# Nine loads of q in 1 KB rows, transposed by float32 products (retention and SiLU block, one core)

## The chip, the cores and the metric

The kernel runs on one core of a Trainium2 chip. The metric is the device time of one execution in microseconds (us); of several runs the median is taken. Below, PE is the matrix engine (TensorE), DVE the vector engine, ACT the scalar engine, POOL the general engine (GpSimd) and SP the engine that issues the DMAs (SyncE).

## What is computed

```python
# q, k, v: (4, 8, 768, 64) float32; w_in: (512, 2048), w_out: (2048, 512), both float64 in memory
gamma = 1.0 - 2.0 ** (-5.0 - np.arange(H, dtype=np.float32))
scale = 1.0 / np.sqrt(D)
for t in range(S):
    state = gamma[None, :, None, None] * state + np.einsum('bhd,bhe->bhde', k[:, :, t], v[:, :, t])
    y[:, :, t] = scale * np.einsum('bhd,bhde->bhe', q[:, :, t], state)
x = y.transpose(0, 2, 1, 3).reshape(B * S, H * D)      # (3072, 512)
h = x @ w_in
g = h * (1.0 / (1.0 + np.exp(-h)))
out = g @ w_out
```

A linear recurrence over the positions of each batch entry and head, and then a two-layer network with SiLU on its 3072 rows.

## The kernel before, in words

**Units.** The recurrence is computed in chunks of 128 positions: 6 chunks by 4 batch entries make 24 units, numbered 0 to 23, chunk by chunk. A unit has a q, a k and a v of 8 heads x 128 positions x 64 numbers, 256 KB each. `load(name, n)` (L148) brings one into SBUF with the position on the partition and (head, number) along it, so that every row of the DMA is one head's 64 numbers, 256 B. Units 0 to 7 have a place of their own (`early`, tile kqv); from unit 8 on they go to the tiles kf, qf and vf, of which qf has two buffers and the others three. All DMAs are issued by SP, one after the other.

**Stages of a unit.** `stage_t(n)` (L461) transposes k and q on PE, each by four transposes of 128 positions x 128 columns (two heads of 64) against the identity matrix (L476), into one PSUM bank each (kp, qp); ACT copies a bank to SBUF (L477, kt and qt: 64 numbers of an even head on the lower 64 partitions, of the odd head on the upper 64, and pair of heads x position along a partition). `scale_k` (L411, L418) and `scale_q` (L420, L423) multiply by powers of gamma on DVE. `stage_s` (L498, L504) forms the sums of k and v, `stage_a` (L508, L514) the scores of k and q in quarters of 64x64, `steps_a` (L518) masks the scores (am, L522) and carries the state (mid, state), and `stage_y` (L543, product L562) forms y. A small POOL memset on `token` (L406) makes the second part of y wait for the first. `steps_y` (L599) and `split_x` (L625) copy y and split it in three parts that go through PE in a reduced float format (xt, L633, L636, L639).

**Weights.** `load_w` (L174) brings in a slice of w_in, 512 KB, by one DMA of 128 partitions (L186) and two of 64 (L188), all in rows of 1 KB; `early_slice` (L244) turns its float64 into float32 and splits it on ACT and DVE (L205 to L224, L121 to L129).

**First layer.** `P(n)` stands for `multiply(c, f)` (L729, L734), twelve products of 128x128 weights by 512 columns into the banks ha and hb, and `CL` for the steps that close it (L742: ACT L744, DVE L749, ACT L754); its result goes to DRAM (`put_g`, L757, L760).

**Order.** PE's instructions go in the order of the program throughout. Up to L976 the other engines and SP do so as well; this early order is written out by hand (L858 to L975): a line there names a unit's stage (T, K, SC, A, Q, YA, YB, X), a step of a weight slice (W), a product (P, CL) or a load. In it units 0 to 8 pass through their stages and the first products (0, 0), (0, 1), (0, 2) and (1, 0) are made. `T(n)` is `stage_t(n)`. Dummy products on zeros (`fill`, `narrow`, L317 and L323) stand in places where PE would wait. Loads stand some units ahead of their use: for instance k and q of unit 10 behind T(8), and v of unit 9 behind T(7). From unit 10 on `halves` (L674) calls the stages between the products of the first layer; units 10 to 12 (ROWS) are transposed in halves of 64 positions (L485). From unit 14 on q and k are transposed by DMA. Then the first layer runs to its end, and the second layer (L1088, L1102) reads its results back from DRAM and multiplies them with w_out.

Of the kernel before, what the change touches and what calls it, by code (L numbers as in the profile page):

```python
# [13 lines left out]
FP32 = mybir.dt.float32  # L14
# [4 lines left out]
AF = mybir.ActivationFunctionType  # L19
# [15 lines left out]
def kernel(  # L35
# [28 lines left out]
    nc = tc.nc  # L64
    B, H, S, D = q.shape
    DM, DF = moe_w_in.shape
    C = 128
    NC = S // C
    HP = H // 2
    KIN = DM // 128  # L70
    NF = DF // 128
# [18 lines left out]
    one = pool("one", 1)  # L90
# [48 lines left out]
    units = [(c, b) for c in range(NC) for b in range(B)]  # L139
    kqv = {"k": {}, "q": {}, "v": {}}  # L140
    EARLY = 2 * B

    FAR = 3 * B + 2
    ROWS = range(2 * B + 2, FAR - 1)
# [3 lines left out]
    def load(name, n):  # L148
        if n >= len(units):
            return  # L150
        c, b = units[n]
        src = {"k": k, "q": q, "v": v}[name]
        if n == 4 * B and name == "k":
            t = conv.tile([128, H, D], FP32, tag="wl", name=f"kf_{n}")
            nc.sync.dma_start(out=t, in_=src[b, :, ds(c * C, C)].rearrange("h t d -> t h d"))
            kqv[name][n] = t
            return
        if n < EARLY:

            if n not in early:  # L160
                early[n] = wpool.tile([128, 3, H, D], FP32, tag=f"w{4 + n}", name=f"kqv_{n}")
            t = early[n][:, "kqv".index(name)]
        else:
            t = ld.tile([128, H, D], FP32, tag=f"{name}f", name=f"{name}f_{n}",
                        bufs=2 if name == "q" else 3)
        nc.sync.dma_start(out=t, in_=src[b, :, ds(c * C, C)].rearrange("h t d -> t h d"))  # L166
        kqv[name][n] = t


# [4 lines left out]
    def load_w(i):  # L174
        if i >= 2 * NF:
            return
        if wide:
            t = stage.tile([128, 2 * DM], U32, tag="wf", name=f"wf_{i}")
            w_in, w_out, n = moe_w_in.bitcast(U32), moe_w_out.bitcast(U32), 256
        else:  # L180
            t = stage.tile([128, DM], FP32, tag="wf", name=f"wf_{i}")
            w_in, w_out, n = moe_w_in, moe_w_out, 128
        if i < NF:
            to = t.rearrange("p (i o f) -> o p i f", o=2, f=n)
            src = w_in[:, ts(i, n)].rearrange("(i o p) f -> o p i f", o=2, p=128)
            nc.sync.dma_start(out=to[0], in_=src[0])  # L186
            for j in range(2):
                nc.sync.dma_start(out=to[1, ts(j, D)], in_=src[1, ts(1 - j, D)])  # L188
        else:
            nc.sync.dma_start(out=t, in_=w_out[ts(i - NF, 128), :])  # L190
        staged[i] = t
# [61 lines left out]
    evac, held, w_sb = [], [], {}  # L253
# [59 lines left out]
    def fill(out, n, start=True):  # L313

        cols = out.shape[-1] // 128
        for _ in range(n):
            nc.tensor.matmul(out, lhsT=zero, rhs=zero.unsqueeze(1).to_broadcast([128, cols, 128]),  # L317
                             start=start, stop=True, skip_group_check=True)

    def narrow(out, n):  # L320

        for _ in range(n):
            nc.tensor.matmul(out[:, :32], lhsT=zero, rhs=zero[:, :32], start=True, stop=True,  # L323
                             skip_group_check=True)

    for n in range(EARLY - 2):
        for name in "kqv":
            load(name, n)
        if n in (0, 3):
            load_w(n // 3)  # L330


    ident = const.tile([128, 128], FP32, tag="ident", name="ident")
# [19 lines left out]
    lgc = const.tile([128, HP], FP32, tag="lgc", name="lgc")  # L353
# [29 lines left out]
    xt, kt, qt, am = {}, {}, {}, {}  # L383
# [8 lines left out]
    def banks(tag, name, n=2):  # L392
        return ps_u.tile([128, n, 512], FP32, tag=tag, name=name)
# [3 lines left out]
    def turn(name):  # L397
        turns[0] += 1
        return ps_h.tile([128, 512], FP32, tag=f"h{turns[0] % 3}", name=name)
# [58 lines left out]
    FILL_FENCE = {0: 2, 2: 2, 3: 2}  # L458
    FILL_P = {(0, 0): 1, (1, 0): 2}

    def stage_t(n):  # L461

        src = kqv["k"][n], kqv["q"].pop(n)
        tp = turn(f"kp_{n}"), banks("q", f"qp_{n}", 1)[:, 0]

        def new(name, to, bufs):
            to[n] = one.tile([128, HP, C], FP32, tag=name, name=f"{name}_{n}", bufs=bufs)
            return to[n]

        made = ("kt", kt, 2), ("qt", qt, 3)  # L470
        if n not in ROWS:
            for i in range(2):
                fill(tp[i], FILL_T.get(n, (0, 0))[i])
                t = tp[i].rearrange("p (a t) -> p a t", a=HP)
                for a in range(HP):
                    nc.tensor.transpose(t[:, a, :], src[i][:, 2 * a : 2 * a + 2, :], ident)  # L476
                evac[:] = [nc.scalar.copy(out=new(*made[i]), in_=t).ins]  # L477
                if n in NARROW_T:
                    narrow(idle[0], NARROW_T[n][i])
            return  # L480
        tp = [t.rearrange("p (i a t) -> p i a t", i=2, a=HP) for t in tp]
        for i in range(2):
            for a in range(HP):
                for o in range(2):
                    nc.tensor.transpose(tp[o][:, i, a, :], src[i][ts(o, D), 2 * a : 2 * a + 2, :],  # L485
                                        ident[ts(o, D), ts(o, D)])
        made = [new(*m) for m in made]
        for o in range(2):
            for i in range(2):
                evac[:] = [nc.scalar.copy(out=made[i][:, :, ts(o, D)], in_=tp[o][:, i]).ins]  # L490
# [326 lines left out]

    sa, ys, asteps, ysteps = {}, {}, {}, {}

    def T(n):  # L820
        stage_t(n)

    def SC(n):
        sa[n] = sc, sums = score_tile(n)
        stage_s(n, sums)
        stage_a(n, sc)
        asteps[n] = steps_a(n, sc, sums)

    def A(n):
        next(asteps[n], None)  # L830

    def YA(n):
        ys[n] = stage_y(n)
        ys[n][0]()
        ys[n][1](0)

    def YB(n):
        ys[n][1](1)
        ysteps[n] = steps_y(n, ys[n][2])

    def X(n):
        next(ysteps[n], None)
# [3 lines left out]
    def W(i, times=1):  # L846
        if i not in slices:
            slices[i] = early_slice(i)
        for _ in range(times):
            next(slices[i], None)  # L850

    def loads(n):
        for name in "kqv":
            load(name, n)

    K, Q = scale_k, scale_q

    idle[:] = [banks("y", "idle")[:, 0]]  # L858
    narrow(idle[0], 39)
    fill(idle[0], 2)  # L860
    narrow(idle[0], 39)
    T(0), K(0)
    nc.scalar.activation(out=token, in_=lgc[:1, :1], func=AF.Silu)
    SC(0), A(0), Q(0), A(0), A(0)
    W(0), W(0), W(0), W(0), W(0)
    YA(0), YB(0), X(0)
    T(1), K(1)
    W(0)
    load_w(2)
    W(0)  # L870
    X(0), X(0)
    SC(1), A(1)
    W(0)
    A(1)
    Q(1), A(1)
    T(2), K(2)
    W(0), X(0)
    W(0), W(0)
    YA(1), SC(2)
    A(2)  # L880
    YB(1), X(1)
    A(2), Q(2), A(2)
    X(1)
    T(3), K(3)
    X(1), X(1)
    YA(2), YB(2), X(2)
    SC(3), A(3), A(3), Q(3), A(3)
    X(2), W(1), W(1)
    X(2), X(2)
    YA(3), YB(3), X(3), X(3)  # L890
    W(1), W(1)
    T(4)
    X(3), X(3)
    K(4)
    W(1), W(1)
    loads(EARLY - 2), loads(EARLY - 1)
    closing = {}

    def P(n):
        c, f = divmod(n, NF)  # L900
        closing[n] = close_steps(c, f, *multiply(c, f))

    def CL(f):
        next(closing[f], None)

    def KA(n):
        t = kqv["k"][n]
        for h in range(H):
            nc.scalar.activation(out=t[:, h, :], in_=t[:, h, :], func=AF.Copy,
                                 scale=gk[:, units[n][0], h : h + 1])  # L910

    P(0)
    next_chunk()
    SC(4)
    CL(0), CL(0), CL(0)
    put_g(0)
    W(1)
    T(5)
    A(4), A(4), Q(4), K(5), A(4)
    W(1), W(1)  # L920
    YA(4), SC(5), YB(4)
    loads(EARLY)
    load_w(3)
    W(2), W(1)
    A(5)
    W(1), W(2), W(2)
    X(4)
    T(6)
    P(1)
    A(5), Q(5), A(5)  # L930
    KA(6)
    W(2), W(2), W(2)
    load("k", EARLY + 1), load("q", EARLY + 1)
    load_w(4)
    W(2)
    CL(1), CL(1)
    W(2)
    YA(5), SC(6), YB(5)
    X(5)
    W(2), W(2)  # L940
    A(6)
    W(2)
    CL(1)
    put_g(0)
    T(7)
    P(2)
    load("v", EARLY + 1)
    K(7), A(6), Q(6), A(6)
    X(4), X(5), X(4), X(4)
    CL(2)  # L950
    YA(6), SC(7), YB(6)
    X(6)
    T(8)
    load("k", EARLY + 2), load("q", EARLY + 2)
    A(7), A(7), Q(7)
    next_chunk()
    K(8), A(7)
    CL(2), CL(2)
    put_g(0)
    X(5), X(5)  # L960
    X(6)
    YA(7), SC(8), YB(7)
    X(7), X(7)
    A(8)
    X(6), X(6)
    T(9)
    load("v", EARLY + 2), load("k", EARLY + 3), load("q", EARLY + 3)
    X(7), X(7)
    A(8), Q(8), A(8)
    P(NF)  # L970
    KA(9)
    CL(NF), CL(NF)
    taken[0] = 3
    begin_w()
    CL(NF)  # L975
# [179 lines left out]
```

## Time and profile before

| | |
|---|---|
| runs | 613.5, 613.05 and 611.95 us, median 613.05 |
| span of the profiled execution, from the first instruction to the last (the profile gives no other time of it) | 612.6 us |
| PE, busy | 600.9 us (98%) |
| weight loads of PE | 495.9 us (81%) |
| DVE, busy | 397.1 us (65%) |
| ACT, busy | 324.5 us (53%) |
| DMA | 144,336 packets, 108.90 MB, of them 101,137 under 512 B |
| granted clock of PE | full throughout |

How to read it: the profile's page gives for each engine the time in which it has an instruction running; PE's instructions are pipelined and their ends modelled, so a busy PE can still have waits in it. The slices cut the span in 40 equal parts of 15.3 us and give the busy share of each in tenths, 9 being 90% or more; the DMA row is the mean share of 16 DMA engines, and can go over 1 in a short stretch. In a timeline a row has start, duration, engine, line, operation, output and inputs; "PEld" is a weight load of PE, "SPq" an issue by SP. The chain of waits is the work that ended last, followed back from the end. A wait row says which engine and line waited for which: us in total, how often, the longest.

### The profile page before, as it was taken

The numbers are of one execution on the slowest core, as the hardware profiler recorded it, in microseconds if no ns is written. First come the engines' busy times: TensorE is split into PE (matmuls) and PEld (weight loads), VectorE is DVE, ScalarE is ACT, GpSimd is POOL, SyncE is SP. The second block draws the span as 40 slices with busy tenths as digits, with TensorE's granted clock in tenths as the row PEclk, the third lists the DMA queues.
The fourth block names the chain that finished last, engine by engine and source line by source line (L and its number), as shares of the span: only waits on it lengthen the run. The fifth ranks groups of instructions, "written<-read, shape, count | busy, mean of one in ns | idle before, by whom it ended". The sixth has DMA issues, their size and how long they took to land.

```text
span 612.6 us, 13713 instructions
## 1 busy us (share of the span) xinstructions
PE 600.9 (98%) x5509; PEld 495.9 (81%) x5509; DVE 397.1 (65%) x672; ACT 324.5 (53%) x598; POOL 32.9 (5%) x89
## 2 busy tenths in 40 slices
PE   8898999999999999999999999999999999999997
PEld 6686788888888888888888888888888888888886
DVE  4797898678886676766689774635545463645631
ACT  7688678678676667676698632212221322313211
POOL 3000020100021111210000000000000000000000
PEclk9999999999999999999999999999999999999999
DMA  9999976586799699998777542623524433433301
GB/s 195 209 199 231 258 214 203 160 254 188 258 231 233 154 263 263 258 291 255 248 249 267 169 138 69 206 69 106 169 72 136 137 110 97 152 123 99 107 1 69
DMA packets 144336, 108.90 MB, mean 178 GB/s; under 512 B 101137, under 2 KB 109585, under 8 KB 144273
## 3 DMA queue, kind: packets, MB, share of 16 engines
q1 hardware_dynamic: 144272, 108.03, 62.3%
q8 instruction: 43, 0.70, 0.5%
q14 instruction: 21, 0.16, 0.1%
HBM read 66.06 MB, written 36.70 MB: 168 GB/s over the span
## 4 chain that ended last, share of the span: by engine, by line
PE 92%; DMA 3%; SPq 2%; DVE 2%; issue 1%; ACT 0%; DVEq 0%
PE ha L734 28%; PE o L1088 21%; PE oa L1088 14%; PE hb L734 14%; PE ob L1088 7%; PE y L562 3%; DMA qf<-in_q_dram 2%; PE sc L504 1%; SPq L166 1%; PE sc L514 1%; DMA kqv<-in_v_dram 1%; SPq L188 1%; PE o L1102 0%; PE oa L1102 0%; PE kp L485 0%
## 5 line engine op out<-in xcount | busy, mean ns | idle before, releaser
L734 PE MATMUL ha<-xt,wi 128*128 128x512 f32 x768 | 193.0, 393 | 0.0
L734 PEld LDWEIGHTS ha<-xt,wi 128*128 128x128 f32 x768 | 142.4, 188 | 30.5 <-DVE xt L636 0.2
L1088 PE MATMUL o<-wo,gs 128*128 128x512 f32 x564 | 143.1, 389 | 0.0
L805 ACT ACTIVATE gs<-gr 128x512 fp32r<-128x512 f32 x96 | 53.2, 621 | 139.0 <-issue 138.0
L1088 PEld LDWEIGHTS o<-wo,gs 128*128 128x128 f32 x564 | 105.9, 188 | 22.0
L807 DVE TENSOR_TENSOR gs<-gr,gs 128x512 fp32r<-128x512 f32 x96 | 62.1, 684 | 94.2 <-ACT gs L805 94.2
L1088 PE MATMUL oa<-wo,gs 128*128 128x512 f32 x376 | 115.7, 389 | 0.0
L749 DVE TENSOR_TENSOR g<-g,hb 128x512 f32<-128x512 f32 x96 | 65.7, 684 | 57.6 <-ACT g L744 42.6
L734 PE MATMUL hb<-xt,wi 128*128 128x512 f32 x384 | 102.7, 389 | 0.0
L734 PEld LDWEIGHTS hb<-xt,wi 128*128 128x128 f32 x384 | 72.1, 188 | 15.1
L1088 PEld LDWEIGHTS oa<-wo,gs 128*128 128x128 f32 x376 | 70.5, 188 | 14.6
L754 ACT ACTIVATE g<-g 128x512 f32<-128x512 f32 x96 | 60.3, 629 | 37.7 <-DVE g L749 37.6
L1088 PE MATMUL ob<-wo,gs 128*128 128x512 f32 x188 | 73.1, 389 | 0.0
L744 ACT ACTIVATE g<-ha 128x512 f32<-128x512 f32 x96 | 56.7, 591 | 28.6 <-PE ha L734 19.8
L808 DVE SCALAR_TENSOR_TENSOR gs<-gs 128x512 fp32r<-128x512 f32 x96 | 62.0, 683 | 0.1
L1088 PEld LDWEIGHTS ob<-wo,gs 128*128 128x128 f32 x188 | 35.3, 188 | 7.4
L205 ACT ACTIVATE ca<-wf 128x512 f32<-128x512 f32 x32 | 21.6, 675 | 6.6 <-DVE cs L218 4.0
L522 DVE TENSOR_TENSOR am<-sc,decay 128x512 f32<-128x512 f32 x24 | 16.5, 687 | 11.4 <-PE sc L514 11.4
L1112 ACT ACTIVATE o<-o 128x512 f32<-128x512 f32 x10 | 6.0, 598 | 33.4 <-PE o L1088 33.0
L218 DVE SCALAR_TENSOR_TENSOR cs<-ca,cs 128x512 uint32<-128x512 uint32 x32 | 22.7, 710 | 0.9
L639 DVE SCALAR_TENSOR_TENSOR xt<-xt 128x512 fp32r<-128x512 f32 x28 | 19.9, 715 | 0.7
L562 PE MATMUL y<-qt,mid 64*64 64x64 f32 x376 | 19.4, 220 | 0.4 <-issue 0.4
(122 smaller groups left out, 562.2 us busy)
## 6 DMA issues: line engine op xcount, KB each, us to landing
gd<-g SPq DMA_DIRECT2D x96, 256.0 KB, 3.7
gr<-gd SPq DMA_DIRECT2D x96, 256.0 KB, 2.7
wf<-in_moe_w_out_dram SPq DMA_DIRECT2D x16, 512.0 KB, 4.7
out_dram<-o SPq DMA_DIRECT2D x23, 256.0 KB, 2.1
wf<-in_moe_w_in_dram SPq DMA_DIRECT2D x16, 256.0 KB, 4.6
wf<-in_moe_w_in_dram SPq DMA_DIRECT2D x32, 128.0 KB, 4.1
kf<-in_k_dram SPq DMA_DIRECT2D x16, 256.0 KB, 4.1
qf<-in_q_dram SPq DMA_DIRECT2D x16, 256.0 KB, 4.1
```

The costliest lines, as they stand in the source:

```text
L205: top = nc.scalar.activation(out=a.bitcast(FP32), in_=hi.bitcast(FP32), func=AF.Abs, scale=2.0 ** -3).ins
L218: nc.vector.scalar_tensor_tensor(out=s, in0=a, scalar=3, in1=s, op0=ALU.logical_shift_left, op1=ALU.bitwise_xor)
L562: i = nc.tensor.matmul(to[ts(e, D), o, a, :], lhsT=lhsT, rhs=rhs, start=key not in started, stop=True, skip_group_check=True).ins
L639: nc.vector.scalar_tensor_tensor(out=x[2], in0=x[1].bitcast(FP32), scalar=-1.0 / EPS, in1=x[0].bitcast(FP32), op0=ALU.mult, op1=ALU.add)
L734: nc.tensor.matmul(hb if i == 2 else ha, lhsT=w_sb[f][:, i, ts(kk, 128)], rhs=xt[c][:, i, kk, :], start=kk == 0 and i != 1, stop=kk == KIN ...
L744: copied[:] = [nc.scalar.activation(out=hs, in_=ha, func=AF.Copy, scale=ONE_E).ins]
L749: taken_out[:] = [nc.vector.tensor_tensor(out=hs, in0=hs, in1=hb, op=ALU.subtract).ins]
L754: nc.scalar.activation(out=hs, in_=hs, func=AF.Silu)
L805: nc.scalar.activation(out=t[:, 0, :], in_=g, func=AF.Copy, scale=HALF)
L807: nc.vector.tensor_tensor(out=t[:, 1, :], in0=g, in1=high, op=ALU.subtract)
L808: nc.vector.scalar_tensor_tensor(out=t[:, 2, :], in0=t[:, 1, :].bitcast(FP32), scalar=-1.0 / EPS, in1=high, op0=ALU.mult, op1=ALU.add)
L1088: nc.tensor.matmul(o, lhsT=g, rhs=wo[f][:, i, :], start=f == 0 and i != 1, stop=f == NF - 1 and i != 0)
```

## The change

Units 1 to 9 are called PACKED; R is 128 x 4 / 128 = 4. Their q is loaded by two DMAs, one for the even heads (j = 0) and one for the odd (j = 1). A partition now holds four consecutive positions of one head of each kind: partition p = 4 u + a holds, at j, positions 4u to 4u + 3 of head 2a + j. Four positions of a head are 1 KB in DRAM, so each DMA moves 128 rows of 1 KB. The loads of k and v, and those of q in other units, stay.

`stage_t` is divided for units 0 to 9 in `stage_k` and `stage_q`, called one after the other where stage_t was called (`T` still names the two). For a packed unit, `stage_q` makes eight float32 products in place of four transposes. For every r (position within the four) and j the 128 partitions x 64 numbers are the weights, and the identity matrix is the moving operand, its columns taken in the order a, u, with a step of four numbers (16 bytes). The output, 64 partitions (lower half for j = 0, upper for j = 1) x 128 columns, goes to PSUM at a x 128 + 4u + r, again in steps of four numbers, so that the bank holds what the transposes left there, and the copy to SBUF is the same. `stage_t` stays for units from 10 on.

The order of all stages, steps and loads written out by hand is unchanged; the lines are only written one call to a line.

```diff
+    PACKED, R = {1, 2, 3, 4, 5, 6, 7, 8, 9}, C * HP // 128
...
-        nc.sync.dma_start(out=t, in_=src[b, :, ds(c * C, C)].rearrange("h t d -> t h d"))
+        rows = src[b, :, ds(c * C, C)]
+        if name == "q" and n in PACKED:
+            rows = rows.rearrange("(a j) (u r) d -> j u a (r d)", j=2, r=R)
+            for j in range(2):
+                nc.sync.dma_start(out=t[:, ts(j, R)].rearrange("p r d -> p (r d)"), in_=rows[j])
+        else:
+            nc.sync.dma_start(out=t, in_=rows.rearrange("h t d -> t h d"))
...
+    def stage_k(n):
+
+        src, u = kqv["k"][n], turn(f"kp_{n}")
+        fill(u, FILL_T.get(n, (0, 0))[0])
+        t = u.rearrange("p (a t) -> p a t", a=HP)
+        for a in range(HP):
+            nc.tensor.transpose(t[:, a, :], src[:, 2 * a : 2 * a + 2, :], ident)
+        evac[:] = [nc.scalar.copy(out=new_t(n, "kt"), in_=t).ins]
+        narrow(idle[0], NARROW_T.get(n, (0, 0))[0])
+
+    def stage_q(n):
+
+        src = kqv["q"].pop(n)
+        to, u = new_t(n, "qt"), banks("q", f"qp_{n}", 1)[:, 0]
+        fill(u, FILL_T.get(n, (0, 0))[1])
+        t = u.rearrange("p (a t) -> p a t", a=HP)
+        if n in PACKED:
+            to_r = u.rearrange("p (a u r) -> p r a u", a=HP, r=R)
+            for r in range(R):
+                for j in range(2):
+                    nc.tensor.matmul(to_r[ts(j, D), r], lhsT=src[:, j * R + r, :],
+                                     rhs=ident.rearrange("p (u a) -> p a u", a=HP),
+                                     start=True, stop=True, skip_group_check=True)
+        else:
+            for a in range(HP):
+                nc.tensor.transpose(t[:, a, :], src[:, 2 * a : 2 * a + 2, :], ident)
+        evac[:] = [nc.scalar.copy(out=to, in_=t).ins]
+        narrow(idle[0], NARROW_T.get(n, (0, 0))[1])
...
+    TK, TQ = stage_k, stage_q
+
     def T(n):
-        stage_t(n)
+        TK(n), TQ(n)
```

More of the change, by code (lines that the diff above doesn't have):

```diff
@@ L324, in narrow @@
                              skip_group_check=True)
[L326 to L330, printed above, removed]
+    load("k",0)
+    load("q",0)
+    load("v",0)
+    load_w(0)
+    load("k",1)
+    load("q",1)
+    load("v",1)
+    load("k",2)
+    load("q",2)
+    load("v",2)
+    load("k",3)
+    load("q",3)
+    load("v",3)
+    load_w(1)
+    load("k",4)
+    load("q",4)
+    load("v",4)
+    load("k",5)
+    load("q",5)
+    load("v",5)
     ident = const.tile([128, 128], FP32, tag="ident", name="ident")
@@ L459, with new_t @@
     FILL_P = {(0, 0): 1, (1, 0): 2}
+    def new_t(n, name):
+        made, bufs = (kt, 2) if name == "kt" else (qt, 3)
+        made[n] = one.tile([128, HP, C], FP32, tag=name, name=f"{name}_{n}", bufs=bufs)
+        return made[n]
+    def stage_k(n):
[23 more added lines that the diff above has]
+        narrow(idle[0], NARROW_T.get(n, (0, 0))[1])
     def stage_t(n):
@@ L472, in stage_t @@
             for i in range(2):
-                fill(tp[i], FILL_T.get(n, (0, 0))[i])
                 t = tp[i].rearrange("p (a t) -> p a t", a=HP)
@@ L477, in stage_t @@
                 evac[:] = [nc.scalar.copy(out=new(*made[i]), in_=t).ins]
-                if n in NARROW_T:
-                    narrow(idle[0], NARROW_T[n][i])
             return
@@ L856 @@
     K, Q = scale_k, scale_q
[L858 to L896, printed above, removed]
     closing = {}
@@ L910, in KA, with warm @@
                                  scale=gk[:, units[n][0], h : h + 1])
+    def warm():
+        nc.scalar.activation(out=token, in_=lgc[:1, :1], func=AF.Silu)
+    idle[:] = [banks("y", "idle")[:, 0]]
+    narrow(idle[0], 39)
+    fill(idle[0], 2)
+    narrow(idle[0], 39)
+    TK(0)
+    TQ(0)
+    K(0)
+    warm()
+    SC(0)
+    A(0)
+    Q(0)
+    A(0)
+    A(0)
+    W(0)
+    W(0)
+    W(0)
+    W(0)
+    W(0)
+    YA(0)
+    YB(0)
+    X(0)
+    TK(1)
+    TQ(1)
+    K(1)
+    W(0)
+    load_w(2)
+    W(0)
+    X(0)
+    X(0)
+    SC(1)
+    A(1)
+    W(0)
+    A(1)
+    Q(1)
+    A(1)
+    TK(2)
+    TQ(2)
+    K(2)
+    W(0)
+    X(0)
+    W(0)
+    W(0)
+    YA(1)
+    SC(2)
+    A(2)
+    YB(1)
+    X(1)
+    A(2)
+    Q(2)
+    A(2)
+    X(1)
+    TK(3)
+    TQ(3)
+    K(3)
+    X(1)
+    X(1)
+    YA(2)
+    YB(2)
+    X(2)
+    SC(3)
+    A(3)
+    A(3)
+    Q(3)
+    A(3)
+    X(2)
+    W(1)
+    W(1)
+    X(2)
+    X(2)
+    YA(3)
+    YB(3)
+    X(3)
+    X(3)
+    W(1)
+    W(1)
+    TK(4)
+    TQ(4)
+    X(3)
+    X(3)
+    K(4)
+    W(1)
+    W(1)
+    load("k",6)
+    load("q",6)
+    load("v",6)
+    load("k",7)
+    load("q",7)
+    load("v",7)
     P(0)
@@ L914 @@
     SC(4)
-    CL(0), CL(0), CL(0)
+    CL(0)
+    CL(0)
+    CL(0)
     put_g(0)
     W(1)
[L918 to L922, printed above, removed]
+    TK(5)
+    TQ(5)
+    A(4)
+    A(4)
+    Q(4)
+    K(5)
+    A(4)
+    W(1)
+    W(1)
+    YA(4)
+    SC(5)
+    YB(4)
+    load("k",8)
+    load("q",8)
+    load("v",8)
     load_w(3)
-    W(2), W(1)
-    A(5)
-    W(1), W(2), W(2)
-    X(4)
-    T(6)
-    P(1)
-    A(5), Q(5), A(5)
+    W(2)
+    W(1)
+    A(5)
+    W(1)
+    W(2)
+    W(2)
+    X(4)
+    TK(6)
+    TQ(6)
+    P(1)
+    A(5)
+    Q(5)
+    A(5)
     KA(6)
-    W(2), W(2), W(2)
-    load("k", EARLY + 1), load("q", EARLY + 1)
+    W(2)
+    W(2)
+    W(2)
+    load("k",9)
+    load("q",9)
     load_w(4)
     W(2)
-    CL(1), CL(1)
-    W(2)
-    YA(5), SC(6), YB(5)
-    X(5)
-    W(2), W(2)
+    CL(1)
+    CL(1)
+    W(2)
+    YA(5)
+    SC(6)
+    YB(5)
+    X(5)
+    W(2)
+    W(2)
     A(6)
@@ L944 @@
     put_g(0)
-    T(7)
-    P(2)
-    load("v", EARLY + 1)
-    K(7), A(6), Q(6), A(6)
-    X(4), X(5), X(4), X(4)
+    TK(7)
+    TQ(7)
+    P(2)
+    load("v",9)
+    K(7)
+    A(6)
+    Q(6)
+    A(6)
+    X(4)
+    X(5)
+    X(4)
+    X(4)
     CL(2)
-    YA(6), SC(7), YB(6)
-    X(6)
-    T(8)
-    load("k", EARLY + 2), load("q", EARLY + 2)
-    A(7), A(7), Q(7)
+    YA(6)
+    SC(7)
+    YB(6)
+    X(6)
+    TK(8)
+    TQ(8)
+    load("k",10)
+    load("q",10)
+    A(7)
+    A(7)
+    Q(7)
     next_chunk()
-    K(8), A(7)
-    CL(2), CL(2)
+    K(8)
+    A(7)
+    CL(2)
+    CL(2)
     put_g(0)
-    X(5), X(5)
-    X(6)
-    YA(7), SC(8), YB(7)
-    X(7), X(7)
-    A(8)
[L965 to L969, printed above, removed]
+    X(5)
+    X(5)
+    X(6)
+    YA(7)
+    SC(8)
+    YB(7)
+    X(7)
+    X(7)
+    A(8)
+    X(6)
+    X(6)
+    TK(9)
+    TQ(9)
+    load("v",10)
+    load("k",11)
+    load("q",11)
+    X(7)
+    X(7)
+    A(8)
+    Q(8)
+    A(8)
     P(NF)
     KA(9)
-    CL(NF), CL(NF)
+    CL(NF)
+    CL(NF)
     taken[0] = 3
```

## The prediction, made before the changed kernel was run

> **What bounds the kernel now.** I read the page's slices first, then the busy time of two stretches, then who waits for whom in the first of them.
>
> ```profile
> span 612.6 us, 13713 instructions
> ...
> PE   8898999999999999999999999999999999999997
> ...
> DMA  9999976586799699998777542623524433433301
> ```
>
> ```profile
> 0.00:60.00 60.00, 52.11 (x1338) 41.96 (x1339) 45.05 (x83) 45.86 (x113) 5.50 (x49) 1.00 0.93 208
> 60.00:600.00 540.00, 540.00 (x4131) 446.73 (x4131) 349.20 (x584) 276.38 (x482) 27.44 (x40) 1.00 0.60 177
> ```
>
> After the times in the second fence: PE, weight loads, DVE, ACT, POOL, granted clock, DMA share, GB/s. From 60 us on PE never rests: whatever comes late or early by then moves the end by as much, and nothing else does. The change touches only the stage before, units 1 to 9; its last transposes of q are at 53 us. There PE rests 60 - 52.1 = 7.9 us and the DMA engines are 93% busy. The waits of that stage which a faster load could end, from two windows (0 to 18 us, then 48 to 60 us):
>
> ```profile
> PE sc L504 <- DMA kqv<-in_v_dram: 1.6, 2, 1.1
> ...
> PE qp L476 <- DMA kqv<-in_q_dram: 0.3, 1, 0.3
> ```
>
> ```profile
> PE kp L485 <- DMA qf<-in_q_dram: 1.1, 1, 1.1
> ...
> PE kp L485 <- DMA kf<-in_k_dram: 0.3, 1, 0.3
> PE qp L476 <- DMA qf<-in_q_dram: 0.3, 1, 0.3
> ```
>
> In the timeline these are: q of unit 1 at 11.66 (0.31), v of unit 2 at 17.73 (1.12), q of unit 9 at 52.73 (0.26), k of unit 10 at 56.98 (0.34) and q of unit 10 at 58.54 (1.09). Unit 0's wait for v comes before any changed load. So **at most 3.1 us can be won**. The rest of PE's rest is dependence on DVE and ACT, and waits put down to "issue".
>
> **The loads.** A q load is 1024 rows of 256 B now and 256 rows of 1 KB after. Two stretches with nearly one kind of row each (256 B, then the 1 KB rows of w_in):
>
> ```profile
> 12.50:16.50 4.00, 4.00 (x117) 3.21 (x117) 3.35 (x7) 2.93 (x6) 0.00 (x0) 1.00 1.18 237
> 101.80:103.20 1.40, 1.40 (x8) 1.17 (x7) 1.40 (x3) 0.93 (x2) 0.00 (x0) 1.00 0.40 127
> ```
>
> At share 1 that is 237/1.18 = 201 and 127/0.40 = 317 GB/s, so 262 KB take 1.30 and 0.83 us: 0.47 us less a load. Two changed loads lie ahead of v of unit 2 (0.9 us), nine ahead of unit 10 (4.2 us). SP issues two DMAs instead of one:
>
> ```profile
> 70.89 0.39 SPq L166 DMA_DIRECT2D qf<-in_q_dram  x1
> ...
> 77.84 1.26 SPq L188 DMA_DIRECT2D wf<-in_moe_w_in_dram  x2
> ```
>
> The nearest row for a 128 KB half is L188, 1.26/2 = 0.63 us; two cost 1.26 + 0.04 between them against 0.39 when nothing is backed up, 0.9 us more, nine times 8.2 us. I take zero: before 60 us the same instruction takes 0.6 to 2.4 us because the DMA engines are behind, and a unit's k, q and v need 0.39 + 1.30 + 0.39 = 2.1 us of SP against 1.30 + 0.83 + 1.30 = 3.4 us of DMA. Were that cover gone, SP would eat the 4.2 us and unit 10 would land as late as now. The q load of unit 10 also needs the buffer of unit 8, which stage_q frees; that comes at about 51 us (below), and 4.1 us to landing gives 55, ahead of its use.
>
> **The products.** The rows, from the chain of waits:
>
> ```profile
> 18.42 0.47 PE sc L514 x32
> ...
> 19.11 0.59 PE kp L476 x4
> ...
> 19.91 0.44 PE qp L476 x4
> ```
>
> Gone: four transposes of 128 columns, 0.44 us, 0.11 each. Added: eight float32 products, 128 rows by 64 columns of weights, 128 columns moving. L514 shows what a float32 product is: 16 calls give 32 instructions, so each is two; 32 take 0.47 us, 14.7 ns each. In the timeline such products start in fours (y at 33.74 to 33.76, 33.80 to 33.82, 33.86 to 33.88), one in each 64x64 quarter every 58 ns. An instruction of 64 columns thus holds its quarter 58 ns; one of 128 columns 0.11 us, as the transposes do. Sixteen of them, two halves of the array side by side, take 8 x 0.11 = 0.88 us. Lower bound: 0.44, if the second pass hid; a gain is excluded, since no more columns stream at once than now. Upper bound: 1.76 without pairing, the same if pairing holds but the 16-byte steps (ident read, PSUM written) halve the rate, 3.5 with both. I take 0.88, because the paired quarters are the nearest row: **+0.44 us a unit**.
>
> Two more switches of array shape: kp costs 0.59 where it follows 64x64 products and 0.44 (qp) where it follows its own shape, so 0.15 a switch. Every unit gets one (k to q); units 4, 6, 7 and 9 a second, since a 128x128 product P follows. So +0.59 for units 1, 2, 3, 5 and 8, +0.74 for 4, 6, 7 and 9: 5.9 us in all. The copy to SBUF (0.58 us, contiguous as before) is unchanged.
>
> The Trainium skill (PSUM — Partial Sum Buffer, Specifications) says that any non-contiguous access pattern slows matmuls significantly; no row here has one, and by it the block is 1.76 us or more. The Trainium skill (TensorE: Matmul & The Clock Gate, Terms) has transposes four times as fast as float32 products; the rows above give 0.11 against 2 x 0.11 for 128 columns, so the trace says twice; by four it would again be 1.76, and its chance is in the first rival's.
>
> **What lies on the path.** Lateness of PE against the trace, walked unit by unit:
> - Units 1, 2: +0.59 - 0.31 (q lands sooner), then +0.59: scores of unit 2 could start at 16.61 + 0.9 = 17.5. v lands at 17.7 - 0.9 = 16.8. So 0.2 early.
> - Unit 3: +0.59, less the 0.17 that the next product waits for mid: 0.2 late. Unit 4: +0.74, 0.95 late.
> - Unit 5: +0.05 only; the products behind it wait for DVE (am, then qt L423) until 33.63. 1.0 late.
> - Unit 6: +0.74; the products behind P wait 0.35 for ACT L909 at 39.73, which itself moves some 0.1: +0.5. 1.5 late.
> - Unit 7: +0.74, 2.2. Unit 8: +0.59 less 0.1 ahead of qt: 2.7.
> - Unit 9: +0.74, less 0.26 (its q) and 0.25 (ha waits for xt L636 at 54.53): 2.95.
> - Unit 10: the waits of 0.34 and 1.09 are gone: 1.5 late.
> Then instructions: 24 more PE instructions a unit, 216 with their loads, on about 2700 before 60 us (1338 + 1339). The "issue" waits of PE between 21 and 52 us are 0.39, 0.43, 0.35 and 0.27; 8% more of 1.44 us is 0.12; as such a wait comes whole or not at all, I take 0.2. Together **+1.7 us**. The profiled execution has a span of 612.6 us, and no other time of it is given; the median of the runs is 613.05, so I add the difference there: 614.8 us. What a measurement of this kernel can tell from no change is about 0.3%, 1.84 us.
>
> **Rivals.**
> - *The steps of 16 bytes, or halves that don't pair* (0.32): the block takes 1.76 us, 0.88 more than in the sum. For: no row shows a strided operand of PE, nor two 128x64 tiles. Against: four quarters do run at once, and float32 streams at half the rate of L734 (512 columns in 1.85/8 = 0.23 us), which leaves time for a step. 9 x 0.88 = 7.9 us more, with some 0.5 hidden at units 6 and 8: 614.8 + 7.4 = 622.2. This is the Trainium skill's PSUM rule at work. Both together (0.04) give 16 us more still.
> - *Not slower: the landing of unit 10 sets the end* (0.15). The price is the block: at 0.44 us with the switches hidden in the "issue" waits, the waits won are 0.9 (v), 0.26, 0.34 and 1.09 = 2.6 us: 610.5. For: the chain runs through one piece of 11.8 us of q loads up to 58.5, and mostly through DVE from 30.7 to 44. Against: PE has no rest from 36 to 48 us. Linear between -2.6 (nothing added) and +1.5 (0.66 a unit), it decides at 0.42 a unit: less is faster.
> - *The rows of 1 KB do not land sooner* (0.05): SP's 0.9 us a load, or two DMAs' fixed costs, eat the 4.2 us. Unit 2 is 0.2 later than in the sum, unit 9's 0.26 stays; unit 10's waits still go, as PE arrives 3 us later. 613.05 + 2.2 = 615.3.
>
> **Chances.** Forecast 0.44, with its own range 613.0 to 616.8 (the walk's hidden parts, 2.4 us, half lost or half more found): faster 0.01, same 0.23, slower 0.20. Strided or unpaired 0.36 with both together, all slower. Landing 0.15: faster 0.12, same 0.03. No gain 0.05: same 0.03, slower 0.02. Sums: faster 0.13, same 0.29, slower 0.58. The range: from 611.2 (most of the landing case) to 622.5 (the strided case's middle); below lie 0.07, above 0.13.
>
> **What would show it.** Loads: packets 144,336 - 9 x 768 = 137,424, q issues of 128 KB, v of unit 2 landing near 16.8. Products: 16 matmuls of 128x64 by 128 columns a unit; pairs starting every 0.11 us confirm 0.88, every 0.22 the strided or unpaired case. Path: PE's waits for q and k of unit 10 gone, the last qp of unit 9 about 3 us later than 53.3, the first y product behind unit 10 at 58.93 + 1.7. The prediction fails if the block isn't 0.88, if DVE rather than PE carries 30 to 54 us, or if PE still waits for q of unit 10.

## The result, and the profile after

The changed kernel takes 622.01 us (median of 4 runs, 621.21 to 622.66) where the kernel before takes 613.27 on the same chip (4 runs, 611.95 to 614.67). The medians lie 8.7 us apart. The measured ratio is 1.0118, interval 1.0078 to 1.0157, which is 7.2 us of 613 and 4.8 to 9.6 by the interval; the quotient of the two medians would be 1.0143, inside that interval. The forecast was 614.8, the range held the time, and the first rival had 622.2. The profiled execution took 621.21 us with a span of 619.4, 6.8 more than the span of before.

From the page of the changed kernel:

```profile
span 619.4 us, 13937 instructions
...
PE   8999999999999999999999999999999999999997
...
DMA  9984776585699899999867552432523433442301
...
DMA packets 137569, 108.92 MB, mean 176 GB/s; under 512 B 92065, under 2 KB 102817, under 8 KB 137505
```

The two stretches, in the columns of the same view of before:

```profile
0.00:60.00 60.00, 58.02 (x1353) 43.82 (x1353) 38.80 (x71) 39.03 (x93) 5.99 (x49) 1.00 0.83 195
60.00:600.00 540.00, 540.00 (x4195) 446.24 (x4195) 356.78 (x596) 283.78 (x502) 28.77 (x40) 1.00 0.61 178
```

In the first 60 us PE rests 2.0 us instead of 7.9, the DMA engines are busy 0.83 instead of 0.93, and DVE and ACT do 6 to 7 us less work by then. PE is at nearly full occupation and behind. All of PE's waits from 9 to 66 us:

```profile
PE y L615 <- issue: 0.3, 1, 0.3
PE y L615 <- POOL token L428: 0.2, 1, 0.2
```

There is no wait for a load among them. And the tile qp (columns: count, duration of one as shortest/median/longest, first and last start, shape), then a stretch of the chain of waits (start, length):

```profile
L508 PE MATMUL qp<-ident,kqv x112: 405/405/423, 11.0 to 49.5; 128*64 128x128 f32 x112
L508 PE MATMUL qp<-ident,qf x32: 406/408/423, 55.4 to 61.6; 128*64 128x128 f32 x32
```

```profile
47.36 0.59 PE kp L494 x4
47.95 1.95 PE qp L508 x16
49.90 2.05 PE ha L787 x8
```

The block of q takes 1.95 us where it took 0.44; kp ahead of it keeps its 0.59. In the timeline the two halves of a pair start 6 to 7 ns apart, so they do run together, but the next pair starts only 0.227 us later. The prediction had 0.11 us for the sum and 0.22 for the rival.

How late PE is follows from the start of kp in each unit:

| start of kp, us, in unit | 2 | 4 | 6 | 8 | 10 |
|---|---|---|---|---|---|
| before | 14.3 | 26.0 | 35.9 | 47.6 | 57.0 |
| the change | 15.2 | 28.5 | 39.8 | 54.8 | 65.2 |
| both operands in order (third run below) | 14.2 | 28.0 | 38.7 | 51.8 | 62.8 |
| new loads, old transposes (fourth run) | 14.1 | 24.6 | 34.5 | 46.7 | 56.2 |

The first y product behind unit 10 starts at 65.86 instead of 58.93, 6.9 us late, and the span grows by 6.8: in the changed kernel what is lost before 60 us is lost at the end, as the prediction read it.

### The profile page after: what moved, and what is told of

Read it like the earlier page. It is cut to its first block, busy times and chain, and to the rows that moved or that the text cites. A ratio compares the mean times of both kernels' runs of the same rounds, so it can differ in the third digit from the quotient of the medians.

```text
span 619.4 us, 13937 instructions
## 1 busy us (share of the span) xinstructions
PE 613.7 (99%) x5617; PEld 503.1 (81%) x5617; DVE 398.4 (64%) x672; ACT 325.1 (52%) x598; POOL 34.8 (6%) x89
## 4 chain that ended last, share of the span: by engine, by line
PE 98%; POOL 0%; ACT 0%; issue 0%; DVE 0%; DVEq 0%; POOLq 0%
PE ha L787 29%; PE o L1247 21%; PE hb L787 14%; PE oa L1247 14%; PE ob L1247 7%; PE y L615 4%; PE qp L508 3%; PE sc L567 2%; PE sc L557 2%; PE kp L494 1%; PE o L1261 0%; PE oa L1261 0%; PE kp L538 0%; PE y L324 0%; ACT decay L368 0%
## 5 line engine op out<-in xcount | busy, mean ns | idle before, releaser
L802 DVE TENSOR_TENSOR g<-g,hb 128x512 f32<-128x512 f32 x96 | 65.7, 685 | 59.0 <-ACT g L797 39.8
L807 ACT ACTIVATE g<-g 128x512 f32<-128x512 f32 x96 | 60.4, 629 | 38.7 <-DVE g L802 38.4
L1272 DVE TENSOR_TENSOR o<-o,o 128x512 f32<-128x512 f32 x10 | 6.8, 688 | 19.3 <-ACT o L1271 19.3
```

The costliest lines, as they stand in the source:

```text
L802: taken_out[:] = [nc.vector.tensor_tensor(out=hs, in0=hs, in1=hb, op=ALU.subtract).ins]
L807: nc.scalar.activation(out=hs, in_=hs, func=AF.Silu)
```

## The experiments

Two theories stood at first: a strided operand halves the rate (and then which, the identity read from SBUF or the output written to PSUM), or the halves only look paired. Later the question was why products at full rate still cost more than their time. Diffs are against the changed kernel unless another is named. Each kernel is compared with the kernel before in runs on its own chip.

### 1. PSUM written in order, identity still read in steps

```diff
-            to_r = u.rearrange("p (a u r) -> p r a u", a=HP, r=R)
+            to_r = u.rearrange("p (r a u) -> p r a u", a=HP, r=R)
...
+            t = u.rearrange("p (r a u) -> p a u r", a=HP, r=R)
+            to = to.rearrange("p a (u r) -> p a u r", r=R)
```

The ACT copy puts the positions in order instead.

> The products read the identity in steps of 16 bytes as in the change, but write 128 neighbouring numbers of PSUM each; the copy by ACT puts them in order. Pairs of products started 0.227 us apart in the changed kernel, where 0.11 was taken. Theory 'step of the write': pairs 0.11 us apart, block of sixteen 0.95 us, time 622.0 - 9 x 1.0 and a little of hidden waits back, 613.5 to 616. Theory 'step of the read': pairs stay at 0.227 us, 622 us. Theory 'two halves with all 128 rows share a feed': 0.227 us, 622 us. The copy by ACT took 0.587 us; if reading PSUM in steps slows it, it shows there.

Measured: 622.79 us, ratio 1.0114 (1.0076 to 1.0152). The tile qp:

```profile
L508 PE MATMUL qp<-ident,kqv x112: 405/405/423, 11.0 to 49.7; 128*64 128x128 f32 x112
```

A product takes the same 405 ns, a pair the same 0.227 us. The step in PSUM was not what it cost. The copy with its reordering took 587 ns, as the plain copy of before did (591).

### 2. Identity read in order, PSUM still written in steps

```diff
-                                     rhs=ident.rearrange("p (u a) -> p a u", a=HP),
+                                     rhs=ident.rearrange("p (u a) -> p u a", a=HP),
...
-            to_r = u.rearrange("p (a u r) -> p r a u", a=HP, r=R)
+            to_r = u.rearrange("p (a u r) -> p r u a", a=HP, r=R)
```

> The products read the identity in order, and write PSUM in steps (512 bytes between neighbours, 16 between rounds of four). 'Step of the read': pairs 0.11 us apart, block 0.95 us, time 613.5 to 616. 'Step of the write': 0.227 us or more, 622 us or more. 'Two halves share a feed': 0.227 us, 622 us.

Measured: 620.28 us, 1.0072 (1.0045 to 1.0099). The tile qp:

```profile
L508 PE MATMUL qp<-ident,kqv x112: 272/273/476, 11.2 to 47.6; 128*64 128x128 f32 x112
```

273 ns in place of 405; pairs start every 0.109 us, and the output still goes to PSUM in steps of 512 bytes from one column to the next and of 16 bytes from one group of four to the next. So the step in the moving operand's read halves the rate and these steps in the write cost nothing. A write in steps of 16 bytes from each column to the next beside a read in order, as the change would have it, was not run. The time stayed above the 613.5 to 616 expected, and run 3, without any step, shows that this is not the write's doing. The Trainium skill has a rule for each: non-contiguous access to PSUM slows matmuls significantly (PSUM — Partial Sum Buffer, Specifications), which this run contradicts for float32 products, and SBUF wants at least two accesses to a line of 16 bytes for full bandwidth (SBUF — State Buffer, Specifications), with which runs 1 and 2 agree: a step of 16 bytes touches a new line with each column.

### 3. Neither in steps

Both edits: the identity as in 2, PSUM as `"p (r u a) -> p r u a"`, the ACT copy puts the positions in order.

> Neither operand has a step; the copy by ACT puts the numbers in order. Either theory of a step: pairs 0.11 us apart, block 0.95 us, and then the prediction's own sum holds: 613.3 + 1.7 = 615.0 us, between 613.5 and 616.5. 'Two halves share a feed': pairs 0.227 us apart, block 2.0 us, 622 us.

Measured: 619.85 us, 1.0069 (1.0041 to 1.0096); 273 ns, pairs every 0.109 us, the block 1.02 us in the chain. That is the block that the prediction had summed, 8 x 0.11 = 0.88 and a switch of 0.15. Yet the kernel is 4.2 us over the one before (0.69% of 613), not 1.7. PE's waits from 9 to 66 us that are put down to "issue", and the longest of them in the timeline:

```profile
PE y L618 <- issue: 3.4, 3, 1.9
PE qp L508 <- issue: 0.7, 1, 0.7
PE sc L570 <- issue: 0.4, 1, 0.4
```

```profile
24.13 0.56 PE L618 MATMUL y<-am,kqv 64*64 64x64 f32 x19
26.62 0.45 PE L618 MATMUL y<-am,kqv 64*64 64x64 f32 x13 [1.93 <-issue]
```

PE stops for 1.93 us in the middle of 32 products of one kind that stand ready, with nothing to wait for. This is the new question: the 4.5 us put down to "issue", where the kernel before has 0.8 in the same window.

The profile is of an execution of 623.95 us, the longest of the eleven. Its first y product behind unit 10 is 4.5 us late (63.40), about what the median lost, but its span is 9.6 us longer. Of the other 5.1 us, 3.4 are waits of PE behind 66 us, most of them for ACT:

```profile
PE hb L790 <- ACT g L800: 3.0, 3, 1.2
```

The profiles of before and of the change have no wait of PE there. Why ACT came late is not shown.

### 4. The loads alone

```diff
-        if n in PACKED:
+        if n in ():
```

in `stage_q`: four transposes, as before.

> The new loads with the old four transposes a unit, so that q of units 1 to 9 comes out in a wrong order: the loads by themselves. By the prediction's walk 2.6 us of waits go (0.9 at v of unit 2, 0.26, 0.34 and 1.09 at units 9 and 10): 610.7 us, 609.7 to 611.7. If the 1 KB rows gain nothing, 613.3 us; if DVE and not PE carries 30 to 54 us, only what comes at unit 10 is won, 612 us.

Measured: 613.2 us, 0.9974 (0.9955 to 0.9994), 1.6 us less than before. The loads do what was said of them: in the profile no wait of PE for a load is left, and the first y product behind unit 10 starts 2.0 us sooner (56.91). The 2.6 us of the prediction's landing case were more than that, though still inside the interval (0.4 to 2.8 us by its bounds). PE's waits put down to "issue" are 2.3 us in this profile, 1.6 of them in one.

### 5. The same columns in fewer instructions

```diff
-            for r in range(R):
-                for j in range(2):
-                    nc.tensor.matmul(to_r[ts(j, D), r], lhsT=src[:, j * R + r, :],
-                                     rhs=ident.rearrange("p (u a) -> p a u", a=HP),
-                                     start=True, stop=True, skip_group_check=True)
+            for j in range(2):
+                nc.tensor.matmul(u[ts(j, D)].rearrange("p (r c) -> p r c", r=R),
+                                 lhsT=src[:, j * R, :],
+                                 rhs=ident.unsqueeze(1).to_broadcast([128, R, 128]),
+                                 start=True, stop=True, skip_group_check=True)
```

The ACT copy is that of 3. A unit has 4 matmuls and 4 weight loads, as many as the transposes had, and streams as many columns as 3.

> As the kernel with both operands flat, but a unit has two float32 products of 512 columns (the identity four times over) in place of eight of 128: PE streams the same columns in the same two halves, 0.9 us a unit, with 4 + 4 instructions on PE instead of 16 + 16. It leaves out three quarters of q (the same quarter is written four times). Theory 'PE's time': what made the flat kernel 0.7% slower is the 0.5 us a block and 0.15 us a switch, so this one is as slow, 0.7%. Theory 'instructions': its longest waits, put down to issue (1.93, 1.14 and 0.74 us), come every 254 matrix instructions, because PE's next block of instructions is not there; with as few instructions as before they shrink to those of before (0.2 to 0.5), and the time is 2 to 3 us shorter than the flat kernel's, 0.2 to 0.4% slower than before.

Measured: 616.15 us, 1.0016 (0.9992 to 1.0039), and y behind unit 10 at 59.62, 0.7 us late. With the PE time of 3, most of the loss of 3 is gone, and PE's "issue" waits in the window are 1.5 us. Each execution is recorded with its mean granted clock, and the gap is not one of the clock: among the executions at 0.999 or 1.0 the medians are 616.1 us here (11 of 12) and 618.3 in run 3 (6 of 11). So the time that products hold PE costs little here, 1.0 us (up to 2.4 by the interval), and the prediction's +1.7 less its 0.2 fits that; what costs the rest goes with the number of instructions.

### 6. Products of 128 columns of weights

```diff
+                nc.tensor.matmul(u[:, ts(r, 128)], lhsT=src[:, 2 * r : 2 * r + 2, :], rhs=ident,
+                                 start=True, stop=True, skip_group_check=True)
```

for each r, in place of the two of 64: 8 matmuls and 8 weight loads a unit, and no switch of array shape. The ACT copy is that of 3.

> Both operands flat, and four products of 128 rows x 128 columns of weights in place of eight of 64 columns (two neighbouring positions of one head together, so q comes out in a wrong order): 0.11 x 8 = 0.87 us of PE a unit as before this step, 8 + 8 instructions, and no switch of array shape between k and q. Against the kernel with two wide products, which has the switch and 4 + 4 instructions: 'PE's time' gives 13 x 0.15 = 1.9 us less here than in the flat kernel and than in the wide one; 'instructions' gives a time between those two, nearer to the wide one.

Measured: 618.86 us, 1.0062 (1.0038 to 1.0087): nearer to 3 than to 5, which the instruction theory had not expected. In its profile "issue" takes 2.6 us by 66 us, the longest wait 1.6, and 1.4 us more in one stop that ends at 199 us; the granted clock of the first 60 us is 0.97. The loss doesn't grow in proportion to the instructions; a few more can bring most of it.

### 7. Units 1 to 3 alone

The kernel of 3 with `PACKED = {1, 2, 3}`.

> Both operands flat and only units 1 to 3 packed, correct. Their products lie before and beside the wait for v of unit 2 (1.12 us). Loads: 3 x 0.47 = 1.4 us less of DMA time ahead of q of unit 10; products: 0.9 us early at the scores of unit 2, then 0.6 to 0.9 late again at unit 3. By the walk 1 to 1.4 us faster than before (0.2%), at most the 0.26% of the loads alone. If the loads only pay when all nine are packed, no difference; if three units' instructions cost as those of nine did, 0.2% slower.

Measured: 616.79 us, 1.0020 (0.9998 to 1.0041). A gain was expected and none came; the time is that of the last case named, 0.2% slower, with an interval that just takes in no change. Its first y product behind unit 10 starts at 58.65, 0.3 us sooner than before. The profile (an execution of 617.09 us, its span 2.7 us longer than that of before) loses 1.7 us behind 66 us: a stop of 1.3 us put down to "issue", which ends at 196 us, and 0.4 us of waiting for ACT.

### 8. The change's products on the old loads

```diff
-        if name == "q" and n in PACKED:
+        if name == "q" and n in ():
```

in `load`.

> The products of the change with the old loads, so that q of units 1 to 9 comes out wrong: the price of the products by themselves. If the loads' 1.6 us (0.26%) add up with the products' price, 1.4 to 1.5% slower than before, where the change is 1.2%. If PE is so late that no load is waited for, the loads are worth nothing beside the products, and this is 1.2% slower too.

Measured: 621.49 us, 1.0108 (1.0079 to 1.0136), against 1.0118 for the whole change. Beside products at half rate the loads are worth nothing that can be measured: PE comes later than nearly every load does, and 0.6 us of waits for old loads are left in this run's profile.

### 9 and 10. More instructions in the kernel before

In the kernel before, in `stage_t`, ahead of q's transposes in units 1 to 9; the first line in run 9, the second in run 10:

```diff
+                if i and 1 <= n <= 9:
+                    narrow(tp[1], 12)
```

```diff
+                if i and 1 <= n <= 9:
+                    fill(tp[1], 2)
```

> The kernel before, with twelve bf16 products of 32 columns on zeros put ahead of q's four transposes in units 1 to 9 (what they write is overwritten): 24 more PE instructions a unit, as many as the change adds, and no other load or product. A narrow product holds PE 34 ns in the trace of before (3.1 us for 91), so twelve are 0.41 us, 3.7 us in nine units, some 2.4 us after the parts that hide. Theory (PE runs short of instructions while the DMA engines are full): beside that the waits put down to issue grow by about 2 to 3 us, so 4.4 to 5.4 us over the kernel before and 2 us or more over the run with two wide products. Rival (instructions cost nothing beyond the time they stream; the full-rate kernel lost its time to something else in its products): 2.4 us over the kernel before, and within 1 us of the run with two wide products.

> The kernel before, with two bf16 products of 512 columns on zeros in the same place: 4 more PE instructions a unit in place of 24, and 0.23 us each by the chain of before (1.85 us for eight), 0.46 us a unit, so slightly more PE time than the twelve narrow ones. Both theories: 4.1 us more PE time, some 2.8 us after the parts that hide. Instruction theory: 2 us or more under the run with twelve narrow products. Rival: equal to it or up to 1 us above it.

Measured: 621.14 us, 1.0112 (1.0075 to 1.0149), with the twelve narrow products; 618.12 us, 1.0063 (1.0037 to 1.0090), with the two wide ones, which hold PE as long. No load, layout or product of the change is in either. Twenty-four more instructions a unit thus cost the kernel before as much as the whole change does, and 3.0 us more than four of the same PE time (0.0049 of the time; put together from the two intervals, 0.0003 to 0.0095).

That difference shows in the granted clock. Its mean was 0.993 to 0.996 in all six executions of run 9, and 0.999 or 1.0 in nine of the twelve of run 10. On average run 9 lost 0.0055, which is some 3.4 us of 617 (an estimate: PE works nearly throughout), as much as lies between the two runs. So these runs don't show that the stops by their own length cost more with 24 instructions than with four; they show that the clock fell more. In run 9's profile it fell twice, each time behind a stop (last section).

PE's waits for the instructions themselves, run 9 and then run 10:

```profile
PE y L564 <- issue: 3.7, 2, 1.9
PE sc L516 <- issue: 0.6, 1, 0.6
```

```profile
PE sc L516 <- issue: 2.2, 2, 2.1
...
PE y L564 <- issue: 1.0, 2, 0.6
```

The longest of each:

```profile
23.45 0.56 PE L564 MATMUL y<-am,kqv 64*64 64x64 f32 x19
25.93 0.45 PE L564 MATMUL y<-am,kqv 64*64 64x64 f32 x13 [1.93 <-issue]
```

```profile
54.08 0.51 PE L516 MATMUL sc<-qt,kt 64*64 64x64 f32 x19
56.64 0.39 PE L516 MATMUL sc<-qt,kt 64*64 64x64 f32 x11 [2.05 <-issue]
```

Run 9 stops where run 3 does, behind the nineteenth of the same 32 products, although its products of q are others. Counted over matmuls and weight loads from the program's start, PE stops behind number 1206 in both; other such stops lie behind 951 or 952 (before, 3, 10), 1713 (3), 2471 to 2477 (3, 4, 9, 10, 12), 2727 (3) and 5777 (6, 7). They are some 254 apart, or a multiple of that. The profile's instruction queue brings pieces of 0.72 MB / 44 = 16 KB, and in ten of the kernels PE went on 1.3 to 1.6 us after the piece that landed last before the end of a stop behind 1205 or 1206 (in 3: PE stopped at 24.7, the piece landed at 25.1, PE went on at 26.6; before: 26.6, 25.5 and 27.06). So it is at the seams between pieces of its program that PE runs dry, mostly in the stage whose DMA engines are 83% to 94% busy. Run 10's profile is of an execution of 622.06 us, well above its median, so its 3.2 us of "issue" may be more than it usually has.

### 11 and 12. New loads, old transposes, q in order by a copy on POOL

```diff
+    def pair_q(n):
+        if n in PACKED:
+            t = early[n - 1][:, 1].rearrange("p (r j) d -> p r j d", j=2)
+            nc.gpsimd.tensor_copy(out=t.rearrange("p r j d -> p j r d"),
+                                  in_=kqv["q"].pop(n).rearrange("p (j r) d -> p j r d", j=2))
+            kqv["q"][n] = t
...
+                nc.tensor.transpose(u[:, ts(r, 128)], src[:, r], ident)
```

The last line stands in place of the products, for each r; PACKED ends at 8, and the ACT copy is that of 3. In run 11 `pair_q(n + 1)` is called in `SC(n)`; in run 12 that of unit 1 is called in `YB(0)` instead.

> The loads of the change for units 1 to 8, one copy of each q on POOL, 128x512 float32, that puts the two heads of a pair side by side (into the slot of the unit before, issued at the scores of that unit), and then four transposes of 128 columns as before, with the ACT copy putting the positions in order: no added PE instruction, q in the right order. POOL is busy 5.5 of the first 60 us, and its one product of this size in the trace of before took 1.04 us (L418). Instruction theory: PE loses nothing, so this keeps what the new loads gave with the old transposes (0.9974), less where q lands just in time and the copy's 1.0 us is waited for (one unit at least, and unit 9 keeps its old load): 0.997 to 1.000, that is 612 to 614. Rival (the products were not what cost the full-rate kernel, but q's new layout and its ACT copy): 1.004 or more.

> As the run before with the copies on POOL, but the copy of unit 1 is issued behind unit 0's token instead of ahead of it. In that run's trace the copy of unit 1 waited for q until 11.22, the token behind it came at 11.81, and PE's products y of unit 0 waited 1.99 us for the token; from then on PE lost nothing more. If that one wait was what the copies cost, 2 us less: 615.2, ratio near 1.001. If the spread of the copies' run (615.2 to 621.2) has another cause, such as instruction waits that fall differently from run to run, the median stays within 1 us of 617.3.

Measured: 617.25 us, 1.0051 (1.0025 to 1.0078), in run 11; 614.38 us, 0.9992 (0.9968 to 1.0017), in run 12. Run 11's POOL in the timeline, then what PE waited for:

```profile
11.22 0.65 POOL L501 COPY kqv<-kqv 128x512 f32<-128x512 f32 x1 [3.83 <-DMA kqv<-in_q_dram]
11.81 0.09 POOL L428 MEMSET token<- 1x1 f32 x1
```

```profile
PE y L620 <- POOL token L428: 2.0, 1, 2.0
```

A small memset that PE needs stood behind a copy that waited for a load. Behind it, the copies (0.61 to 0.78 us) were hidden, and moving one of them took the median down by 2.9 us, more than the 2.0 of that wait. The granted clock is part of it. Behind that wait run 11's profile has a clock of 0.80, 0.50 and 0.85 from 12 to 18 us, 1.7 us of PE lost. Its twelve executions go by their clock: the five at 0.997 took 615.2 to 615.8 us, the seven at 0.993 or 0.994 took 617.2 to 621.2. In run 12 nine of twelve were at 0.999 or 1.0. Run 11's ratio is in the rival's range, 1.004 or more, but run 12 has the same loads and the same ACT copy and is not slower, so these are not the cause.

Run 12 has the loads and the right order of q, no added PE instruction, and is level with the kernel before. Where the 1.6 us of run 4 went was not measured apart. Its profile, of an execution of 617.3 us, has a wait of 1.2 us for the copy of unit 1 and 2.2 us of "issue" on PE, 2.0 of it at one seam; and unit 9 keeps its old load. No version with q in order beat the kernel before by a measurable amount.

## Why the prediction was right or wrong, point by point

**What bounds the kernel: right for the change.** PE doesn't rest after 60 us, and lateness before is lateness at the end: 6.9 us at the first y product behind unit 10, 6.8 in the span. It doesn't hold for every kernel here: the profile of run 3 has 3.4 us of PE's waits behind 66 us, those of runs 6 and 7 have 1.4 and 1.7.

**The loads: right in kind.** The packets fell by 6,767, 752 a load where 768 were counted. SP's second issue was hidden, as was said. Two rows of SP in the changed kernel, its two issues of a unit's q in one row:

```profile
5.86 1.50 SPq L171 DMA_DIRECT2D kqv<-in_q_dram  x2
...
28.35 1.24 SPq L171 DMA_DIRECT2D kqv<-in_q_dram  x2
```

They take 0.6 to 0.75 us each, as L188 does, and no wait of PE for a load was left. All the waits for loads that could be won were won (run 4: -1.6 us, where -2.6 was the most that the landing case gave), but the loss beside them is larger.

**The products: the step that failed.** "I take 0.88, because the paired quarters are the nearest row" mis-sized the block: it took 8 x 0.227 = 1.82 us, 1.95 with its switch, where the sum has 0.88 and 1.03. The pairing was right, and a pair of 0.109 us was right for operands in order (run 3). The row of the quarters reads its moving operand without a step, and had nothing to say on the step of 16 bytes in the identity. The prediction had named that step, on the read and on the write together, and priced it at 1.76; run 1 and run 2 take it apart: the step in the read does it, with the step in the write or without. Its argument against, that float32 at half the rate of L734 "leaves time for a step", is refuted by 405 against 273 ns. By the rival's sum the time was 622.2, and 622.01 came. The mechanism is the rival's; that the two agree to 0.2 us is partly luck. That sum has PE 1.7 + 7.4 = 9.1 us late, the profile shows 6.9 at unit 10, and the ratio gives 7.2, so the walk found some 2 us too little that hides. And the range held the time because its upper edge lay at the middle of the rival's case.

**Transposes against products: right.** Four transposes took 0.44 us and the same columns as full-rate products 0.88, twice. The pairs of 0.109 us in run 3 stand for that.

**The instructions: the second step that failed.** "I take 0.2", from 8% more of 1.44 us of "issue" waits. Of these, 0.35 and 0.27 are waits of weight loads (PEld at 45.54 and 51.43) while PE worked; PE's own are 0.39 and 0.43. At full rate (run 3) PE's were 4.5 us in the profile of the longest execution, and by the ratio the kernel came out 2.5 us above the forecast although its block was as summed. The mistake was to take such waits as proportional to the instructions. They lie at seams 254 instructions apart, each costs nothing or up to 2 us, and 216 more short instructions bring PE to the seam before the piece is there (runs 9 and 3; in 3 PE is at number 1206 at 24.7 us, before at 26.6). The change itself hardly shows it, 0.3 us; that its products are so slow that the pieces arrive in time is likely, but was not tested. So the rival's sum was met without that term. The Trainium skill (Runtime: NRT & Kernel Launch, Instruction fetch mechanics) describes refills in blocks of 256 instructions and calls their cost mostly hidden; the spacing of 254 agrees, the stops of 1.9 to 2.1 us in runs 3, 9 and 10 do not.

**What stays open.** That fewer instructions cost less is measured with 5 against 3, at equal granted clock too. With 9 against 10 the interval just leaves zero out, and the difference is one of the clock. That the pieces come late because the DMA engines are full was only argued: no run emptied them. Run 6 shows that the loss is no simple function of the count.

## What to carry to other kernels

Give a float32 product its moving operand in order, and put the reordering on the side where it is free: here the write to PSUM, in the steps of run 2, or the ACT copy, each without a measurable cost. Look for the row that has the same access pattern before taking the row of the same shape. Where PE is fed small instructions while the DMA engines are full, count its instructions as a cost apart from their time, and expect it in jumps at fixed places in the program.

## What the runs showed of the hardware that was not expected

After a stop of about 2 us the granted clock fell to half for some 3.4 us in some profiles. Run 2, then run 9, both after a stop of 1.9 us that ended near 26:

```profile
26.00:28.00 2.00, 1.65 (x32) 1.20 (x32) 1.29 (x3) 0.00 (x0) 0.09 (x1) 0.80 0.84 204
28.00:30.00 2.00, 2.00 (x16) 1.67 (x16) 0.64 (x1) 1.89 (x4) 0.00 (x0) 0.50 0.97 271
30.00:32.00 2.00, 2.00 (x16) 1.60 (x13) 1.34 (x3) 1.46 (x5) 0.00 (x0) 0.85 1.01 242
```

```profile
28.00:30.00 2.00, 2.00 (x17) 1.75 (x13) 1.29 (x2) 1.99 (x4) 0.00 (x0) 0.50 1.10 266
30.00:32.00 2.00, 2.00 (x8) 1.58 (x7) 0.70 (x2) 1.34 (x5) 0.00 (x0) 0.65 1.02 218
```

Run 9 once more, after a stop of 1.73 us that ended at 55.35:

```profile
54.00:56.00 2.00, 0.65 (x24) 0.65 (x27) 1.97 (x4) 1.97 (x6) 0.00 (x0) 0.82 0.54 122
56.00:58.00 2.00, 2.00 (x86) 2.00 (x83) 0.09 (x1) 0.00 (x0) 0.09 (x1) 0.50 1.01 252
```

The clock is the column after POOL; from 58 to 60 us it is 0.83. Run 2 lost 0.2 x 2 + 0.5 x 2 + 0.15 x 2 = 1.7 us of PE at full rate, run 9 in the first two rows shown 0.5 x 2 + 0.35 x 2 = 1.7, and from 54 to 60 us 0.36 + 1.0 + 0.34 = 1.7 again. At half clock a loss of 1.7 us is 3.4 us of time. Run 3 had a stop as long at 24.7 to 26.6, run 10 one of 2.05 us and run 12 one of 1.97 us, and behind these the clock stayed at 1.00. What decides it is not shown.

So one missed seam can cost its 2 us, and 1.7 more. This is part of why executions of one kernel differ, as runs 9 and 11 show above, and not all of it: in run 3 the six executions at 0.999 or 1.0 alone spread from 617.0 to 623.95 us.
